# Second MLP layer with its weights stationary, router scores from its column sums, and whole-row gathers for the first two expert blocks

## Chip, cores and metric

One core of a Trainium2 chip runs the kernel. The metric is the device time of one execution in microseconds; times given are medians of several executions, and the profile is of one execution.

## What is computed

Three layers on 1792 tokens of 768 values, in float32. The kernel works with fp32r: a number is split into a high and a low part, and a product is made of three matmuls (high x high, high x low, low x high).

```python
scores = scale * np.matmul(q, k.transpose(0, 1, 3, 2)) - np.log(S)     # 4 x 12 heads, S 448, d 64
attn_out = np.matmul(1.0 / (1.0 + np.exp(-scores)), v)                 # -> x[1792, 768]
h = x @ w_in                                                           # w_in 768 x 2048
x = (np.maximum(h, 0.0) + alpha * np.minimum(h, 0.0)) @ w_out          # w_out 2048 x 768
logits = x @ w_gate                                                    # 8 experts
expert_idx = np.argmax(logits, axis=1)
gate_w = probs[np.arange(N), expert_idx]                               # softmax of the logits
for e in range(E):
    mask = expert_idx == e
    out[mask] = gate_w[mask, None] * (np.maximum(x[mask] @ w1[e], 0.0) @ w2[e])   # F 1024
```

## The kernel before

The five engines are in-order queues: TensorE (PE), VectorE (DVE), ScalarE (ACT), GpSimd (POOL) and SyncE (SP), which issues most DMAs. The order on each is the order in which the program is written (a manual schedule); no planner changes it.

**MLP.** The tokens are four groups, three of 512 and one of 256. The 2048 hidden values are eight chunks of 256. `mlp1` makes h of one chunk and group in columns (hidden value by partition, token along the row) with the weights stationary; ACT and DVE make the activation and split it into `gh` and `gl`. `mlp2` (L365) multiplies by w_out: for each tile of 128 tokens the activation is the stationary operand and 384 columns of w_out are the moving one, two halves of six matmuls (L377 to L379), and DVE adds the result to `acc[ti]`, 128 tokens by 768 (L384). In the last chunk the finished tile is stored to `x2d` in DRAM (L386). `x2d` keeps a token as four quarters of 192 values and one more for the gate.

**Routing.** It is spread between the MLP's last pieces by hooks, calls that run between matmuls. `logits` (L415) takes two tiles at a time: 12 PE transposes (L422), copies by ACT and DVE (L424, L425), 24 matmuls with the router's weights (L432) and one small sum matmul (L438). `choose` (L451) finds the expert, `gates` (L460) the gate; `ranks` (L469) counts tokens by expert with matmuls. The first 8 tiles (groups 0 and 1, the early tokens) are ranked first, so that block 0, 128 tokens of one expert, can be gathered and computed while the rest is routed; the late tiles follow, and then the remaining blocks. `block0_ids` and `block_ids` make lists of token numbers with matmuls; `quarter_rows` (L548) makes of a list the numbers of the quarter rows, with a DVE op that rounds the list to float16 (L556) and four matmuls (L559).

**Experts.** A block is gathered by four indirect DMAs on POOL (`gather`, L723), one for each quarter, so that a DVE transpose of 32 x 32 pieces (`tx`, L747) turns 128 tokens by 768 into columns; ACT and DVE split them (L749, L750). `gate_of` (L729) copies the gates on POOL. `moe1` and `moe2` are the expert's two layers; block 0's are cut in halves (`moe1_halves`, `moe2_halves`) with routing between them. `block_experts` (L597) finds on POOL which expert each block has; ACT, DVE and SP read that row to decide which weights to load and split (`next_w`, `next_split`). `split_w1` and `split_w2` split block 0's and block 1's weights into high and low parts, ACT the high one, DVE the low one (L669 to L691). The tag `raw` has two SBUF buffers, which hold the transposed copies of `logits` and, later, of `tx`.

The order of the main program around the change (L966 to L1075) is: chunks 0 to 5; then mlp1(6,2), router, mlp2(7,1), choose and gates for tiles 0 to 3, mlp1(6,3), router, mlp2(6,2), choose and gates for tiles 4 to 7, mlp1(7,2) with the ranks in its middle, mlp2(6,3) with block 0's ids and gather, mlp1(7,3), mlp2(7,2), mlp2(7,3), the late router work between the halves of expert 0's first layer, the late ranks, its second layer with `block_ids`, gathers of blocks 1 and 2, `block_experts`, and then blocks 1, 2, 3 and on.

## Time and profile before

| what | value |
|---|---|
| median of 3 executions | 950.84 us (950.5 to 951.27) |
| profiled execution | 950.54 us, span 948.5 us from first to last instruction |
| mean granted clock of PE | 0.991 |
| PE busy | 931.7 us, 98% of the span |
| DVE, ACT, POOL busy | 552.5, 353.0, 159.3 us (58%, 37%, 17%) |

The busy time of an engine is the union of its instructions. Matmuls overlap one another, so the duration of one (340 ns with 384 columns) is longer than the distance to the next. The granted clock is the share of TensorE's full clock. Idle time of an engine matters only where PE waits for it, so PE's waits are the thing to read, with the stretches of lower clock.

### The profile page before, as it was taken

The page shows a single profiled execution, that of the slowest core. Times are in us where ns is not written, and L with a number is a line of the kernel's source. Part 1 is how long each engine was busy: PE and PEld are TensorE (multiplying, and loading weights), DVE is VectorE, ACT ScalarE, POOL GpSimd, SP SyncE. Part 2 cuts the span into 40 slices and gives each one's busy share as a digit, 9 for nine tenths or more (in the row PEclk, how much of TensorE's full clock was granted, in tenths as well). Part 3 has the DMA queues.
Part 4 walks back from the last instruction along what each step waited for, and adds up shares of the span by engine and source line. Part 5 has one row for each costly group of instructions (what it writes and reads, how often), then busy time and mean ns, then how long its engine had stood idle before and what let it go on. Part 6 is the DMA issues. An engine that isn't in the chain of part 4 may idle for free. (4 is left out here: it accounts for less than half of the span.)

```text
span 948.5 us, 14230 instructions
## 1 busy us (share of the span) xinstructions
PE 931.7 (98%) x5437; PEld 767.8 (81%) x5437; DVE 552.5 (58%) x976; ACT 353.0 (37%) x561; POOL 159.3 (17%) x210
## 2 busy tenths in 40 slices
PE   9999999999999999999999999898999999999996
PEld 3333338989999899998998989886889989989986
DVE  3454413467777677786867734686397552327841
ACT  5776762223222222223222232343366512116710
POOL 0000000000000000000000000336547362342651
PEclk9999999999999999999999999898999999999999
DMA  7755500011121112112211041730478411057400
GB/s 237 193 202 167 204 1 1 1 50 50 50 67 50 51 55 59 54 52 54 63 50 50 22 96 35 297 86 22 179 298 312 171 61 40 25 182 284 171 19 30
DMA packets 38593, 97.09 MB, mean 102 GB/s; under 512 B 12761, under 2 KB 20825, under 8 KB 35440
## 3 DMA queue, kind: packets, MB, share of 16 engines
...
q8 instruction: 45, 0.74, 0.3%
q14 instruction: 36, 0.29, 0.1%
...
## 5 line engine op out<-in xcount | busy, mean ns | idle before, releaser
L377 PE MATMUL y<-wo,gh 128*128 128x384 f32 x448 | 152.4, 340 | 0.0
L379 PE MATMUL y<-wo,gl 128*128 128x384 f32 x448 | 151.3, 338 | 0.0
L378 PE MATMUL y<-wo,gh 128*128 128x384 f32 x448 | 151.3, 338 | 0.0
L384 DVE TENSOR_TENSOR acc<-y,acc 128x768 f32<-128x768 f32 x98 | 93.2, 952 | 18.3 <-PE y L379 18.3
L353 ACT ACTIVATE r<-h 128x512 f32<-128x512 f32 (+1 forms) x64 | 34.8, 543 | 167.5 <-PE h L351 164.0
L699 POOL MEMSET xg<- 128x772 f32 x4 | 2.9, 744 | 554.5 <-PE xt L422 554.5
L355 DVE SCALAR_TENSOR_TENSOR t<-r,alpha,t 128x512 f32<-128x512 f32 (+1 forms) x64 | 43.8, 684 | 86.5 <-ACT t L354 86.5
L377 PEld LDWEIGHTS y<-wo,gh 128*128 128x128 f32 x448 | 84.5, 189 | 1.2 <-issue 0.4
L378 PEld LDWEIGHTS y<-wo,gh 128*128 128x128 f32 x448 | 84.6, 189 | 0.8
L379 PEld LDWEIGHTS y<-wo,gl 128*128 128x128 f32 x448 | 84.6, 189 | 0.0
L723 POOL DMA_INDIRECT xg<-x2d,rt_qids x72 | 79.0, 1097 | 23.3 <-issue 20.8
L758 PE MATMUL f<-w_b,bh 128*128 128x512 f32 x192 | 77.2, 402 | 3.7 <-ACT bh L749 3.7
L243 ACT ACTIVATE a<-sc,bias 128x896 f32<-128x896 f32 x72 | 67.5, 1015 | 25.9 <-PE sc L252 25.9
L349 PE MATMUL h<-xa,wi 128*128 128x512 f32 x192 | 75.1, 391 | 0.0
L351 PE MATMUL h<-xa,wi 128*128 128x512 f32 x192 | 74.8, 390 | 0.0
L350 PE MATMUL h<-xa,wi 128*128 128x512 f32 x192 | 74.7, 389 | 0.0
L349 PE MATMUL h<-xb,wi 128*128 128x512 f32 (+1 forms) x192 | 65.1, 339 | 0.0
L350 PE MATMUL h<-xb,wi 128*128 128x512 f32 (+1 forms) x192 | 64.9, 338 | 0.0
L351 PE MATMUL h<-xb,wi 128*128 128x512 f32 (+1 forms) x192 | 64.8, 338 | 0.0
L357 DVE TENSOR_TENSOR gl<-t,gh 128x512 fp32r<-128x512 f32 (+1 forms) x64 | 40.1, 626 | 41.4 <-ACT gh L356 41.4
L826 PE MATMUL f<-w,hh 128*128 128x384 f32 x180 | 61.9, 344 | 0.0
L768 ACT ACTIVATE hr<-f 128x1024 f32<-128x1024 f32 x16 | 16.4, 1027 | 119.2 <-PE f L765 83.4
(256 smaller groups left out, 1854.3 us busy)
## 6 DMA issues: line engine op xcount, KB each, us to landing
...
xg<-x2d,rt_qids POOLq DMA_INDIRECT x72
out_dram<-ye,rt_ids POOLq DMA_INDIRECT x18
```

What stands on the lines that cost most here:

```text
L243: nc.scalar.activation(a, pt[:, :, :S], AF.Sigmoid, bias=bias, scale=scale)
L349: nc.tensor.matmul(pt[:, :n], wh[:, ks], a, start=(k == 0), stop=False)
L350: nc.tensor.matmul(pt[:, :n], wh[:, ks], b, start=False, stop=False)
L351: nc.tensor.matmul(pt[:, :n], wl[:, ks], a, start=False, stop=(k == HP - 1))
L355: nc.vector.scalar_tensor_tensor(tj, rj, alpha_sb[:, f:f + 1], tj, op0=ALU.mult, op1=ALU.add)
L377: nc.tensor.matmul(pt[:, nh, :HN], gh[:, j, ts], wh[:, ns], start=(j == 0), stop=False)
L378: nc.tensor.matmul(pt[:, nh, :HN], gh[:, j, ts], wl[:, ns], start=False, stop=False)
L379: nc.tensor.matmul(pt[:, nh, :HN], gl[:, j, ts], wh[:, ns], start=False, stop=(j == 1))
L384: nc.vector.tensor_tensor(dst, pt[:, :, :HN], dst, ALU.add)
L723: nc.gpsimd.indirect_dma_start(out=ex["xg"][b % 4][:, q, :], out_offset=None, in_=rows, in_offset=bass.IndirectOffsetOnAxis(ap=at, axis=0) ...
L758: nc.tensor.matmul(pt[:, n, :], bh[:, k, :], h[n], start=(k == 0), stop=False)
L826: nc.tensor.matmul(pt[:, n, :HN], a, h[:, ns], start=(k == 0), stop=False)
```

## The change

- `mlp2` holds 128 x 128 slices of w_out stationary and moves the activations of a whole group (512 or 256 tokens). The sums come out in columns: `acc[g]` is [128, 6, n], and DVE adds two of the six column chunks at a time (128 x 1024 for 512 tokens).
- `logits` takes a whole group and multiplies the columns directly: no transposes and no copies ahead, 24 matmuls for four tiles, one small sum matmul.
- The rows of `x2d` must now be made. For the 8 early tiles `rows_out` does it on DVE, by a 32 x 32 transpose of 128 x 768 that writes every sixth word, with four stores of 96 KB. For the 6 late tiles `rows_turned` does it on PE (6 transposes) with two ACT copies and one store. Both use the two `raw` buffers.
- `x2d` is [1792, 768]; the gates have a DRAM tensor of their own, and `gate_of` is an indirect DMA of 128 values in place of four POOL copies. Three setup DMAs go.
- Blocks 0 and 1 are gathered by whole rows, one indirect DMA each, and turned by 6 PE transposes with two ACT and two DVE ops. So block 0 needs no quarter ids. The quarter ids of the other blocks, the gather of block 2, `block_experts`, `second_block` and `third_ids` move behind the third of ten runs of block 0's second-layer generator `s2`.
- The hidden-weight splits, the memsets of `xg` and block 0's w2 splits move some places; w1 has another layout in DRAM, and tiles that reused places of `acc` are pieces of the groups.

```diff
-        acc = cx["acc"]
-        t0, n = groups[g]
+        acc = cx["acc"][g]
+        n = groups[g][1]
         gh, gl = gbuf.pop((c, g))
-        for i in range(n // P):
-            ti = t0 // P + i
-            ts = slice(i * P, (i + 1) * P)
-            pt = psum2(f"y{c}_{ti}")
-            for nh in range(2):
-                ns = slice(nh * HN, (nh + 1) * HN)
+        for i in range(HP // 2):
+            pt = psum2(f"y{c}_{g}_{i}")
+            for z in range(2):
+                ks = slice((2 * i + z) * P, (2 * i + z + 1) * P)
                 for j in range(2):
                     wh, wl = w_need("o", 2 * c + j)
-                    nc.tensor.matmul(pt[:, nh, :HN], gh[:, j, ts], wh[:, ns], start=(j == 0), stop=False)
-                    nc.tensor.matmul(pt[:, nh, :HN], gh[:, j, ts], wl[:, ns], start=False, stop=False)
-                    nc.tensor.matmul(pt[:, nh, :HN], gl[:, j, ts], wh[:, ns], start=False, stop=(j == 1))
-            dst = acc[ti].rearrange("p (a n) -> p a n", a=2)
+                    nc.tensor.matmul(pt[:, z, :n], wh[:, ks], gh[:, j, :n], start=(j == 0), stop=False)
+                    nc.tensor.matmul(pt[:, z, :n], wl[:, ks], gh[:, j, :n], start=False, stop=False)
+                    nc.tensor.matmul(pt[:, z, :n], wh[:, ks], gl[:, j, :n], start=False, stop=(j == 1))
+            dst = acc[:, 2 * i:2 * i + 2, :]
             if c == 0:
-                nc.vector.tensor_copy(dst, pt[:, :, :HN])
+                nc.vector.tensor_copy(dst, pt[:, :, :n])
             else:
-                nc.vector.tensor_tensor(dst, pt[:, :, :HN], dst, ALU.add)
-            if c == NCH - 1:
-                nc.sync.dma_start(out=x2d[ti * P:(ti + 1) * P, :, :DQ], in_=acc[ti].rearrange("p (g c) -> p g c", g=G))
-            w_step(2)
+                nc.vector.tensor_tensor(dst, pt[:, :, :n], dst, ALU.add)
+            w_step(3)
...
+    def rows_out(g, i):
+        src = cx["acc"][g][:, :, i * P:(i + 1) * P].rearrange("p k (t j) -> p t k j", j=Q)
+        rows = main.tile([P, G, DQ], F32, tag="raw", bufs=2, name=f"rows{g}_{i}")
+        nc.vector.transpose(rows.rearrange("p t (i k) -> p t k i", k=HP), src)
+        t0 = groups[g][0] + i * P
+        for t in range(G):
+            dst = x2d[t0 + t * Q:t0 + (t + 1) * Q].rearrange("j (g c) -> g j c", g=G)
+            nc.sync.dma_start(out=dst, in_=rows[:, t, :])
...
+    def rows_turned(g, i):
+        src = cx["acc"][g][:, :, i * P:(i + 1) * P]
+        pt = psum2(f"rows{g}_{i}")
+        for k in range(HP):
+            nc.tensor.transpose(pt[:, k // 4, (k % 4) * P:(k % 4 + 1) * P], src[:, k, :], ident)
+        rows = main.tile([P, DM], F32, tag="raw", bufs=2, name=f"rows{g}_{i}")
+        by_chunk = rows.rearrange("p (r k) -> p k r", k=HP)
+        for z, n in ((0, 4), (1, 2)):
+            nc.scalar.activation(by_chunk[:, 4 * z:4 * z + n, :], pt[:, z, :n * P].rearrange("p (k m) -> p k m", k=n), AF.Copy)
+        t0 = groups[g][0] + i * P
+        nc.sync.dma_start(out=x2d[t0:t0 + P], in_=rows)
...
+    def logits(g):
+        acc, n = cx["acc"][g], groups[g][1] // P
+        pl = psum1(f"lg{g}")
+        for k in range(HP):
+            for q in range(n):
+                nc.tensor.matmul(pl[Q * q:Q * (q + 1), :P], wg[:, k, :], acc[:, k, q * P:(q + 1) * P], start=(k == 0), stop=(k == HP - 1))
...
-        nc.vector.tensor_scalar(rt["qid0"], quarter_rows(pid, 1, "qids0"), quarter, None, op0=ALU.add)
...
+    def quarter_ids():
+        pq, idf = psum2("qids")[:, 0, :G * TMAX], rt["idf"]
+        for q in range(G):
+            nc.tensor.matmul(pq[:, q * TMAX:(q + 1) * TMAX], rt["spread"][:, q, :], rt["idh"], start=True, stop=True)
+        nc.vector.tensor_scalar(idf, pq, 0.0, 16384.0, op0=ALU.is_equal, op1=ALU.mult)
+        nc.vector.scalar_tensor_tensor(rt["qids"].rearrange("p q b -> p (q b)"), pq, quarter, idf, op0=ALU.add, op1=ALU.add)
...
+    def indirect_in(dst, src, at):
+        nc.gpsimd.indirect_dma_start(out=dst, out_offset=None, in_=src, in_offset=at, bounds_check=src.shape[0] - 1, oob_is_err=False)
...
+        if b < 2:
+            indirect_in(ex["xg"][b % 4], x2d[:XA if b == 0 else NT], offs(b))
+            return
...
+        indirect_in(rt["gate"][:, b % 4:b % 4 + 1], gated[:XA if b == 0 else NT], offs(b))
...
+        if b < 2:
+            pt = ps2("x", f"tx{b}")
+            for k in range(HP):
+                nc.tensor.transpose(pt[:, k // 4, (k % 4) * P:(k % 4 + 1) * P], xg.rearrange("p (r k) -> p k r", k=HP)[:, k, :], ident)
+            parts = [(pt[:, z, :n * P].rearrange("p (k m) -> p k m", k=n), slice(4 * z, 4 * z + n)) for z, n in ((0, 4), (1, 2))]
+            for src, d in parts:
+                nc.scalar.activation(bh[:, d, :], src, AF.Copy)
+            for src, d in parts:
+                nc.vector.tensor_tensor(bl[:, d, :], src, bh[:, d, :].bitcast(F32), ALU.subtract)
+            return
...
-        mlp2(c1, 1, at(lambda: run(lg[0], lg[2]), lambda: run(lg[0], lg[2]), lambda: run(lg[2])))
+        mlp2(c1, 1, at(lambda: (run(lg[0]), rows_out(0, 0)), lambda: rows_out(0, 1), lambda: rows_out(0, 2)))
         choose(0, 4)
         gates(0, 4)
-        mlp1(c0, 3)
-        run(lg[4])
-        mlp2(c0, 2, at(lambda: run(lg[4], lg[6]), lambda: run(lg[4], lg[6]), lambda: run(lg[6])))
+        mlp1(c0, 3, at(lambda: rows_out(0, 3)))
+        run(lg[1])
+        mlp2(c0, 2, at(lambda: (run(lg[1]), rows_out(1, 0)), lambda: (rows_out(1, 1), rows_out(1, 2)), lambda: rows_out(1, 3)))
...
+        mlp2(c1, 2, lambda i: split_w1(next(split1)))
+        mlp2(c1, 3, at(lambda: split_w1(next(split1)), lambda: (run(lg[2]), rows_turned(2, 0)),
+                       lambda: (split_w1(next(split1)), rows_turned(2, 1))))
+        moe_tiles_h()
+        split2 = iter(range(K2))
+        s1 = moe1_halves(0)
+        run(lg[2])
+        tx(0)
+        rows_turned(2, 2)
+        run(lg[3])
+        split_w1(next(split1))
+        rows_turned(2, 3)
+        run(s1, s1, lg[3])
+        rows_turned(3, 0)
+        rows_turned(3, 1)
         moe_w2()
         for z in range(1, 4):
             new["xg"](z)
+        for _ in range(3):
+            split_w2(next(split2), 0)
+        run(s1, s1, s1, s1)
...
         gather(1)
-        gate_of(0)
-        gather(2)
         for k in range(K2):
             split_w2(k, 1)
-        block_experts()
-        second_block()
-        third_ids()
-        for _ in range(TXAT):
+        for n in range(TXAT):
             run(s2)
+            if n == 2:
+                quarter_ids()
+                gather(2)
+                block_experts()
+                second_block()
+                third_ids()
```

What moves in the engines' queues, at the three places that the prediction speaks of (names with numbers are buffers):

DVE ahead of the early ranks, from the middle of mlp2(6,2) to the op that makes the one-hot experts `rt_oh`, which the ranks read. Before:

```order
L425 COPY xtr_0_4973<-xt_0_4966 128x256
L425 COPY xtr_1_4983<-xt_1_4976 128x256
L384 TENSOR_TENSOR acc_1270<-y_9_4986,acc_1270 128x768
L439 COPY rt_L<-lb_5000 128x16
L384 TENSOR_TENSOR acc_1271<-y_10_5018,acc_1271 128x768
L439 COPY rt_L<-lb_5032 128x16
L384 TENSOR_TENSOR acc_1272<-y_11_5035,acc_1272 128x768
L454 TENSOR_REDUCE rt_mx<-rt_L 128x4
L455 TENSOR_TENSOR rt_eq<-rt_L,rt_mx 128x32
L456 TENSOR_TENSOR rt_eq<-rt_eq,e_65 128x32
L457 TENSOR_REDUCE rt_ix<-rt_eq 128x4
L458 TENSOR_TENSOR rt_oh<-e_65,rt_ix 128x32
```

With the change:

```order
L439 COPY rt_L<-lb_4686 128x32
L385 STREAM_TRANSPOSE rows_0_4689<-acc_1255 128x4x6x32
L374 TENSOR_TENSOR acc_1256<-y_2_1_4695,acc_1256 128x1024
L385 STREAM_TRANSPOSE rows_1_4709<-acc_1255 128x4x6x32
L385 STREAM_TRANSPOSE rows_2_4715<-acc_1255 128x4x6x32
L374 TENSOR_TENSOR acc_1256<-y_2_2_4721,acc_1256 128x1024
L385 STREAM_TRANSPOSE rows_3_4735<-acc_1255 128x4x6x32
L454 TENSOR_REDUCE rt_mx<-rt_L 128x4
L455 TENSOR_TENSOR rt_eq<-rt_L,rt_mx 128x32
L456 TENSOR_TENSOR rt_eq<-rt_eq,e_66 128x32
L457 TENSOR_REDUCE rt_ix<-rt_eq 128x4
L458 TENSOR_TENSOR rt_oh<-e_66,rt_ix 128x32
```

The copies for the router (L425) are gone, and row transposes stand between the adds, three of them between the first add's copy of the scores and the last add, one behind it, all ahead of choose.

POOL from block 1's gather to the start of `block_experts`. Before:

```order
L723 DMA xg_5451<-x2d,rt_qids 128x193 x4
L729 COPY rt_gate<-xg_5153 32x1 x4
L723 DMA xg_5453<-x2d,rt_qids 128x193 x4
L601 TENSOR_TENSOR rt_bend<-rt_bst,rt_nbf 1x8
L602 TENSOR_TENSOR rt_late<-rt_bst,blk 1x168
```

With the change:

```order
L725 DMA pieces_4845<-x2d,rt_ids 128x768
L725 DMA pieces_5237<-x2d,rt_qids 128x192 x4
L600 TENSOR_TENSOR rt_bend<-rt_bst,rt_nbf 1x8
L601 TENSOR_TENSOR rt_late<-rt_bst,blk 1x168
L602 TENSOR_SCALAR rt_late<-rt_late 1x168
```

Block 1's gather is one DMA (128 x 768), the gate copies are gone from here, and block 2's four quarter gathers still stand ahead of `block_experts`.

DVE after `block_ids`. Before, the quarter ids are made at once:

```order
L556 TENSOR_SCALAR rt_idh<-ids 128x21
L586 TENSOR_SCALAR rt_idf<-qids 128x84
L587 SCALAR_TENSOR_TENSOR rt_qids<-qids,quarter,rt_idf 128x84
L589 TENSOR_SCALAR rt_idf<-ids 128x21
L590 SCALAR_TENSOR_TENSOR rt_ids<-ids,rt_idf 128x21
L691 TENSOR_TENSOR w2l_5445<-raw_e,w2h_5444 128x384
```

With the change, the block's token ids come first (just ahead of this piece), and the quarter ids at its end:

```order
L690 TENSOR_TENSOR pieces_5235<-raw_e,pieces_5235 128x384
L1075 TENSOR_TENSOR hl_5141<-th_1_5340,hh_5139 128x512
L690 TENSOR_TENSOR w_0_5229<-raw_e,w_0_5229 128x384
L690 TENSOR_TENSOR w_1_5230<-raw_e,w_1_5230 128x384
L690 TENSOR_TENSOR w_2_5231<-raw_e,w_2_5231 128x384
L690 TENSOR_TENSOR w_3_5232<-raw_e,w_3_5232 128x384
L690 TENSOR_TENSOR w_4_5233<-raw_e,w_4_5233 128x384
L690 TENSOR_TENSOR w_5_5234<-raw_e,w_5_5234 128x384
L690 TENSOR_TENSOR pieces_4847<-raw_e,pieces_4847 128x384
L690 TENSOR_TENSOR pieces_5235<-raw_e,pieces_5235 128x384
L566 TENSOR_SCALAR rt_idf<-qids 128x84
L567 SCALAR_TENSOR_TENSOR rt_qids<-qids,quarter,rt_idf 128x84
```

The quarter ids, which block 2's gather waits for, moved behind the weight subtractions (L690).

## Rows read from the trace of the kernel before

**Rows 1.** The page, part 1: busy us, share of the span, instructions.

```profile
PE 931.7 (98%) x5437; PEld 767.8 (81%) x5437; DVE 552.5 (58%) x976; ACT 353.0 (37%) x561; POOL 159.3 (17%) x210
```

**Rows 2.** List of waits of PE, 540 to 700 us: total, times, longest.

```profile
PE f L758 <- ACT bh L749: 3.7, 1, 3.7
PE qids L559 <- DVE rt_idh L556: 3.4, 2, 3.1
```

**Rows 3.** Busy time by stretch: length, engines, granted clock (PEclk), DMA share, GB/s.

```profile
600.25:607.15 6.90, 5.84 (x25) 5.84 (x26) 3.10 (x12) 0.00 (x0) 3.50 (x4) 0.51 1.01 425
654.85:661.75 6.90, 5.22 (x12) 4.13 (x13) 3.29 (x3) 1.87 (x3) 5.88 (x10) 0.51 0.08 16
547.69:591.33 43.64, 43.64 (x339) 39.66 (x339) 19.75 (x48) 12.69 (x27) 0.74 (x1) 1.00 0.24 57
591.33:630.37 39.04, 35.40 (x259) 33.12 (x258) 24.70 (x58) 12.97 (x23) 15.06 (x15) 0.91 0.65 233
630.37:645.28 14.91, 14.29 (x106) 11.48 (x107) 13.66 (x44) 9.41 (x21) 2.35 (x3) 1.00 0.03 2
645.28:667.37 22.09, 18.00 (x76) 14.91 (x76) 11.66 (x26) 5.73 (x12) 16.87 (x31) 0.85 0.10 23
```

**Rows 4.** Timeline of PE: start us, duration of one or of a run.

```profile
522.75 0.34 PE L377 MATMUL y<-wo,gh 128*128 128x384 f32 x1
...
531.13 0.40 PE L349 MATMUL h<-xa,wi 128*128 128x512 f32 x1
...
539.31 0.34 PE L377 MATMUL y<-wo,gh 128*128 128x384 f32 x1
...
569.64 0.28 PE L349 MATMUL h<-xb,wi 128*128 128x256 f32 x1
...
573.95 1.47 PE L422 MATMUL xt<-ident,acc 128*128 128x128 f32 x12
...
577.44 0.86 PE L432 MATMUL lg<-xtr,wg 128*32 128x128 f32 x24
578.24 1.53 PE L422 MATMUL xt<-ident,acc 128*128 128x128 f32 x12
579.52 0.42 PE L377 MATMUL y<-wo,gh 128*128 128x384 f32 x1
```

**Rows 5.** Groups, lines and one timeline row of DVE, ACT and SP: count, durations (ns by line).

```profile
L384 DVE TENSOR_TENSOR acc<-y,acc 128x768 f32<-128x768 f32 x98 | 93.2, 952 | 18.3 <-PE y L379 18.3
...
L747 DVE STREAM_TRANSPOSE xt<-xg x17: 1542/1640/1682, 654.1 to 916.5; 128x768 f32<-128x768 f32 x17
...
L355 DVE SCALAR_TENSOR_TENSOR t<-r,alpha,t 128x256 f32<-128x256 f32 x4 | 1.9, 485 | 4.0 <-ACT t L354 4.0
...
588.28 0.18 DVE L454 TENSOR_REDUCE rt_mx<-rt_L 128x4 f32<-128x32 f32 x1
...
589.16 0.19 DVE L458 TENSOR_TENSOR rt_oh<-e,rt_ix 128x32 f16<-128x32 f32 x1
...
L424 ACT ACTIVATE xtr<-xt 128x512 f32<-128x512 f32 x14 | 8.0, 594 | 8.4 <-PE xt L422 8.2
...
L386 SPq DMA_DIRECT2D x2d<-acc x14: 512/513/572, 543.8 to 625.5; - x14
```

**Rows 6.** Timeline from block_ids to block 2: PE, POOL, DVE, PE.

```profile
651.17 1.10 POOL L723 DMA_INDIRECT xg<-x2d,rt_qids  x1 [0.30 <-issue]
...
658.40 0.19 POOL L601 TENSOR_TENSOR rt_bend<-rt_bst,rt_nbf 1x8 f32<-1x8 f32 x1
...
665.67 0.29 POOL L618 TENSOR_SCALAR rt_row<-rt_late 1x21 int32<-1x21 f32 x1
...
654.05 1.54 DVE L747 STREAM_TRANSPOSE xt<-xg 128x768 f32<-128x768 f32 x1 [1.63 <-DMA xg<-x2d,rt_qids]
...
656.53 0.79 PE L758 MATMUL f<-w_b,bh 128*128 128x512 f32 x1 [3.68 <-ACT bh L749]
...
667.37 0.40 PE L758 MATMUL f<-w_b,bh 128*128 128x512 f32 x1
```

More of the change, by code (lines that the diff above doesn't have):

```diff
@@ L62 @@
     DQ = DM // G
-    x2d = dram.tile([NT, G, DQ + 1], F32, name="x2d")
+    x2d = dram.tile([NT, DM], F32, name="x2d")
+    gated = dram.tile([NT, 1], F32, name="gated")
     def ctile(name, shape, dt=F32):
@@ L98, in setup_routing @@
         nc.sync.dma_start(out=wg[:, :, 0:E], in_=w_gate)
-        none = pool.tile([P, NTT], F32, tag="none", bufs=1, name="none")
-        nc.gpsimd.memset(none, 0.0)
         yield
-        for g in range(1, G):
-            nc.sync.dma_start(out=x2d.rearrange("(t p) g c -> p t g c", p=P)[:, :, g, DQ:DQ + 1], in_=none.unsqueeze(2))
-            yield
         for n, (dst, src) in enumerate(todo):
@@ L546, in late_places @@
         rt["s"] += place(so, rt["lo"], NE, n - POOLN) + on_pool
-    def quarter_rows(pid, n, name):
-        if "spread" not in rt:
-            rt["spread"] = main.tile([P, G, P], F16, tag="dm", bufs=1, name="spread")
-            nc.vector.tensor_scalar(rt["spread"].rearrange("p q (g s) -> p q g s", g=G),
-                                    slot.rearrange("p (q s) -> p q s", q=G).unsqueeze(2).to_broadcast([P, G, G, Q]),
-                                    part, None, op0=ALU.is_equal)
-        with nc.allow_low_precision(reason="multiples of 4 up to 7168 are exact in float16"):
-            nc.vector.tensor_scalar(rt["idh"][:, :n], pid, float(G), None, op0=ALU.mult)
-        pq = psum2(name)[:, 0, :G * n]
-        for q in range(G):
-            nc.tensor.matmul(pq[:, q * n:(q + 1) * n], rt["spread"][:, q, :], rt["idh"][:, :n], start=True, stop=True)
-        return pq
     def block0_ids():
@@ L590, in block_ids @@
         nc.vector.scalar_tensor_tensor(rt["ids"], pid, -1.0, idf, op0=ALU.add, op1=ALU.add)
+        with nc.allow_low_precision(reason="multiples of 4 up to 7168 are exact in float16"):
+            nc.vector.tensor_scalar(rt["idh"], pid, float(G), None, op0=ALU.mult)
     def third_ids():
@@ L682, in moe_w2 @@
             else:
-                parts.append(tuple(cx["mp"].tile([P, DM], F32R, tag="acc", bufs=NTT, name=f"w2{x}_{k}") for x in "hl"))
+                parts.append(tuple(piece(k - 5, 2 * (k == 6) + z) for z in range(2)))
         ex["w2"] = parts
@@ L691, in split_w2, with piece @@
         nc.vector.tensor_tensor(l[:, s], src, h[:, s].bitcast(F32), ALU.subtract)
+    big = {}
+    def piece(g, i):
+        if g not in big:
+            n = groups[g][1] // P
+            big[g] = cx["mp"].tile([P, n, DM], F32R if g in (1, 2) else F32, tag=f"acc{g}", bufs=1, name=f"pieces{g}")
+        return big[g][:, i, :]
     def moe_tiles_a():
-        acc_t = lambda n, dt, c=DM: cx["mp"].tile([P, c], dt, tag="acc", bufs=NTT, name=n)
         ex["xg"], ex["bx"], ex["y"] = {}, {}, {}
         def xg(z):
-            ex["xg"][z] = acc_t(f"xg{z}", F32, G * (DQ + 1)).rearrange("p (q c) -> p q c", q=G)
+            ex["xg"][z] = piece(*((0, z) if z < 2 else (3, z - 2)))
             nc.gpsimd.memset(ex["xg"][z], 0.0)
         def bx(z):
-            ex["bx"][z] = [acc_t(f"b{x}{z}", F32R).rearrange("p (k m) -> p k m", k=HP) for x in "hl"]
+            ex["bx"][z] = [piece(1 + z, 2 * z + i).rearrange("p (k m) -> p k m", k=HP) for i in range(2)]
         def y(z):
-            ex["y"][z] = acc_t(f"ye{z}", F32)
+            ex["y"][z] = piece(0, 2 + z)
         ex["new"] = dict(xg=xg, bx=bx, y=y)
@@ L741, in tx @@
     def tx(b):
+        xg = ex["xg"][b % 4]
         bh, bl = ex["bx"][b % 2]
[L744 removed]
+        if b < 2:
[8 more added lines that the diff above has]
+            return
+        if "xt" not in ex:
             ex["xt"] = main.tile([P, HP, P], F32, tag="raw", bufs=2, name="xt")
[L746 to L748 removed]
+        t = ex["xt"]
+        nc.vector.transpose(t.rearrange("p k (q s) -> p k q s", q=G), xg.rearrange("p (q i k) -> p k q i", q=G, k=HP))
         nc.scalar.activation(bh, t, AF.Copy)
@@ L949 @@
         cx["mp"] = ctx.enter_context(tc.tile_pool(name="mlp", bufs=1, side="right", reuse_waits="tile"))
-        cx["acc"] = [cx["mp"].tile([P, DM], F32, tag="acc", bufs=NTT, name=f"acc{t}") for t in range(NTT)]
+        cx["acc"] = [cx["mp"].tile([P, HP, n], F32, tag=f"acc{g}", bufs=1, name=f"acc{g}") for g, (_, n) in enumerate(groups)]
         nc.vector.tensor_scalar(alpha_sb, alpha_sb, -1.0, None, op0=ALU.mult)
@@ L961 @@
         routing_tiles()
-        lg = {a: logits(a) for a in range(0, NTT, 2)}
+        lg = [logits(g) for g in range(4)]
         def at(*acts):
```

85 lines of the change are left out of this document (22 added, 63 removed).

## The prediction

> **What bounds the kernel now.** The page comes first: PE is busy 98% of the span [rows 1], so only PE's own work, its waits and its clock can move the time. PE's list of waits between 540 and 700 us comes next. Two matter: 3.1 us (3.4 in two waits) for the quarter ids of block 0, which VectorE (DVE) has not rounded yet, and 3.7 us for block 1's transposed tokens [rows 2]. I call them A and B. The table by stretch shows what else they cost: right behind each, PE runs 6.9 us at a granted clock of 0.51, the lower of its two levels (1.2 of 2.4 GHz), with 5.84 and 5.22 us of it busy. At full clock that work takes half as long, so A and B cost another 2.9 and 2.6 us [rows 3]. All other work up to block 3 is nearly gapless and is priced by the distance between starts [rows 4], not by the longer duration of one matmul.
>
> **MLP second layer.** From 522.75 us on, three stretches follow one another: 48 matmuls of 384 columns, 36 of 512, and 48 of 384 again; the first two took 8.38 and 8.18 us [rows 4]. The change turns the 48x384 of a 512-token group into 36x512, the very shape of the 8.18 us stretch (the first layer's, with weights stationary), so -0.20 us. For the 256-token group 24x384 (half of 8.38, 4.19) become 36x256; such a run took 4.31 us (569.64 to 573.95), +0.12. Per chunk 3 x -0.20 + 0.12 = -0.48, times 8 = -3.8 us: **-3.5** before chunk 6 group 2, -0.4 in the next stage, nothing after it. The Trainium skill, TensorE: Matmul & The Clock Gate, § Back-to-back issue gap, states N/2.4 + 2.5 ns from start to start for an isolated pair; by it 48x384 (7.80 us) and 36x512 (7.77) cost the same, and the edit would give about 0.5 us in place of 3.8 (an estimate from that page). The rows disagree, with 227 ns for 512 columns and 175 for 384, so I take them. DVE's adds grow from 128x768 (0.95 us [rows 5]) to 128x1024, by size 1.27, but three replace four: nothing, while PE is the longer.
>
> **Early routing** (chunk 6 group 2 to the first ranks matmul, 43.64 us [rows 3]). 48 transposes go: 12 took 1.28 us with the switch of type (578.24 to 579.52), so -5.1. Of four sets of 24 router matmuls (0.80 us each, 577.44 to 578.24) two go, -1.6; two small sum matmuls with their switches -0.4; two groups of the second layer -0.4; and +0.5 for copies that now follow the router matmuls at once: **-7.0**.
>
> **A new wait at the ranks.** Before, the last op of choose that the ranks need began at 589.16 and took 0.2, and the ranks started at 591.33, where two stretches meet: 2.0 us to spare [rows 3, 5]. Now eight row transposes stand on DVE ahead of it. The nearest row is the same opcode on the same size, 128x768, 1.54 to 1.68 us; I take 1.58. It reads with a stride and writes densely, the new one reads densely and writes every sixth word: bounds 1.0 us (the 0.95 us add of that size) and 3.2 (twice the row). From the end of the first column pair of chunk 7 group 1, DVE has 6 adds x 1.2, 8 x 1.58, choose (588.28 to 589.35, 1.1), gates (about the same), choose again (1.1), four ops of the 256-token group (0.49 each at most) and about 0.5 of copies: 25.6 us, and some 1.0 of waits for ScalarE and for stores. PE has two pairs (5.5), 36x256 (4.3), router (0.9), 36x512 (8.2), 18x512 (4.1) and small waits (1.0): 24.0. So PE waits **2.6 us** where it had none. Of the stores: four take 4 x 0.51 us to issue on SP [rows 5], and a quarter gather released DVE 1.8 us after its issue had ended (651.17 + 1.10 to 654.05 [rows 6]), so a buffer is free again some 4.2 us after its transpose. There are two, so a third transpose in quick succession waits about 1 us, which is in the 1.0.
>
> **From the ranks to expert 0's first matmul** (39.04 us [rows 3]). A goes: 3.2 of wait, 0.4 of quarter-id matmuls, 2.9 of half clock, -6.5. Late router work: 36 transposes become 24 of rows and 6 of block 0's tokens, and half the router matmuls go, -1.3. New: 2.6 at the ranks; 3.2 of half clock behind it, if the clock falls as at A, some 2.2 us after PE's last start, and for 6.9 us; 1.1 at chunk 6 group 3, whose third pair wants a PSUM buffer that the late DVE still holds; 1.7 at expert 0, where ScalarE's copies of rows (0.59 for 512 columns [rows 5], two a tile) stand before the one that frees its PSUM, held up by the same two buffers; small waits of before, -0.8. Sum **0.0**.
>
> **To the block ids** (14.91 us [rows 3]). Two row tiles (12 transposes) +1.3, router work and its switches -1.4. choose for the late tiles now stands behind ScalarE's copies of tiles (3,0) and (3,1), three weight copies, and DVE's three subtractions: by the same durations 9.6 us from expert 0's start, and PE is there at 6.8: **wait 2.9**, half clock behind it 3.1, old waits -0.6. Sum **+5.3**.
>
> **Blocks 1 and 2.** Call I the end of the block ids, 645.28, where the last two stretches meet [rows 3]. Block 1 started at 656.53 [rows 6], I + 11.25. Now its single gather goes out before any quarter ids (I + 2), lands near I + 4.7, is turned on PE inside expert 0's second half, and block 1 starts near I + 8.5. **B is gone there**, but the next thing is late. Gather 2 now follows quarter ids that stand behind eight weight subtractions, to I + 6.4. Four issues of 1.35 us each end at I + 11.8, and POOL's block_experts then takes 658.40 to 665.96, 7.6 us: the row of experts is ready at I + 19.4, before at I + 20.7. ScalarE's branch reads it, and block 2 started 1.4 us later (667.37); so now I + 20.8 against I + 22.1. PE ends block 1 at I + 16.7: a **new wait of 4.1 us** before block 2, with 2.5 of half clock inside it. Net -1.3 + 2.5 = **+1.2**. Block 3's weights start from the same row of experts, 1.3 us earlier, so they are in time.
>
> **At nothing:** the gate by an indirect DMA (one POOL issue for four copies, wanted a step later), three setup DMAs fewer, 32 stores on SP for 8 (16 us of issue in 28). If a cover fails, 1 to 2 us.
>
> **Sum:** -3.5 - 7.0 + 0.0 + 5.3 + 1.2 = -4.0. The profiled execution took 950.54 us (span 948.5 and 2.0 around it), 0.30 below the median of 950.84. 950.54 - 4.0 = **946.5**.
>
> **Rivals.**
> - *The new waits are too short for the clock to fall* (chance 0.26). They are 2.6 to 4.1 us, and the falls of before came 2.2 to 2.4 us after PE's last start. Without three half-clock stretches (3.2 + 3.1 + 2.5) the time is 937.7; without the waits at the ranks and choose too, 932.2. For it: a transpose nearer 1.0 us. Against: 3.1 us sufficed at A.
> - *DVE bounds the stage before the ranks: slower* (0.18). Place: the eight row transposes, all in line before choose. Each us more of one is 8 us at the ranks. It decides from 4.0 / 8 = 0.5 us more, 2.1 us a transpose; at 3.2 us the time is 959.5. For it: a write stride of 24 bytes, which no row has. The Trainium skill, SBUF — State Buffer, § Door 1: The DMA port swizzle, says that accesses which cross to a new 16-byte line pay a penalty, which is the rule behind this rival. Against: the reads of the row cross likewise, and it took 1.6 us.
> - *The change gives little back* (0.14): the second layer no faster than before, +3.8, and stores that hold their buffer 0.5 us longer: about 950.8.
> - The forecast as worked out: 0.42.
>
> **Numbers.** A measurement of this kernel tells 0.2%, 1.9 us, from no change. Faster: the forecast and the first rival, 0.67 (0.01 of them spill over); same 0.15; slower 0.18. The range goes down to the middle of the first rival, 935.5, and up past no change into the slower one, 953; some 0.2 lies beyond.
>
> **What would show it.** Starts 0.227 us apart in the second layer and 8.18 us a group; the ranks' first matmul 10.5 us earlier than 591.33; PE waits at the ranks, at the late ranks, and at block 2 on ScalarE, none at quarter ids; a granted clock of 0.5 behind each of the three. The forecast is wrong if a row transpose differs from 1.6 us by over 0.5, if a store holds its buffer over 6 us, or if block 1 waits for its gather.

## The result and the profile after

The changed kernel takes **961.59 us** (median of 4 runs, 959.78 to 962.84) against 950.67 for the kernel before in the same comparison: a ratio of 1.0125, with a 95% interval of 1.0098 to 1.0153. It is slower by 10.9 us where 946.5 was forecast, and lies outside the range. The profiled execution took 962.06 us, its span 960.3.

PE is busy for 929.2 us, 2.5 less than before [rows 1]. So the 11.8 us by which the span grew, and 2.5 more, are time in which PE has no work running. PE's list of waits, kernel after, 540 to 700 us (total, times, longest), answers to [rows 2]:

```profile
PE rank L477 <- DVE rt_oh L458: 14.2, 2, 12.3
PE f L778 <- ACTq L923: 3.2, 1, 3.2
PE lg L432 <- ACT t L345: 3.1, 1, 3.1
```

The waits A and B of before (quarter ids, block 1's tokens) are gone, as forecast. In their place PE waits 12.3 us for choose ahead of the ranks, where 2.6 was forecast. The table by stretch, kernel after (columns as in [rows 3]), has the four stretches of [rows 3] (the border between the last two is here the first matmul of the block ids, at 644.40 in the kernel before), then the one from block 2 to block 3, and last the three stretches of lower clock, each begun in one of the new waits or right behind it:

```profile
547.72:588.01 40.29, 37.21 (x264) 30.70 (x262) 20.90 (x31) 7.21 (x16) 0.74 (x1) 1.00 0.17 38
588.01:637.31 49.30, 35.88 (x286) 31.53 (x285) 31.36 (x69) 16.06 (x29) 11.39 (x11) 0.86 0.60 186
637.31:654.38 17.07, 15.25 (x79) 12.54 (x79) 10.07 (x36) 10.91 (x20) 3.76 (x5) 0.90 0.26 93
654.38:674.86 20.48, 16.83 (x98) 14.04 (x97) 10.79 (x28) 6.54 (x15) 12.06 (x24) 0.99 0.10 25
674.86:696.85 21.99, 20.70 (x100) 17.75 (x101) 5.12 (x6) 6.37 (x8) 10.96 (x11) 0.93 0.53 192
...
592.50:606.30 13.80, 5.75 (x22) 4.59 (x22) 9.13 (x28) 1.83 (x4) 0.00 (x0) 0.51 0.31 89
...
647.10:650.90 3.80, 3.80 (x15) 3.15 (x13) 3.35 (x16) 1.09 (x3) 1.42 (x2) 0.55 0.12 5
...
674.50:677.60 3.10, 2.74 (x7) 2.16 (x8) 0.00 (x0) 1.03 (x1) 2.31 (x3) 0.50 0.35 127
```

The stretch from the ranks to expert 0's first matmul grew from 39.04 to 49.30 us: 10.3 us, of a loss of 11.8 in all. What makes DVE late there is told by line 385, the row transposes (durations as min/median/max):

```profile
L385 DVE STREAM_TRANSPOSE rows<-acc x8: 1537/1576/1643, 561.8 to 598.0; 128x768 f32<-128x768 f32 x8
its engine sat idle before it (us, times) until:
  DMA x2d<-rows: 8.5, 4
  issue: 5.8, 1
```

A transpose took 1.58 us, exactly the value taken. But DVE stood still for 14.3 us ahead of five of the eight. DVE's timeline shows where, in three rows behind that of the first transpose (the other two that waited, at 589.66 and 598.03, did so for 1.55 us each):

```profile
561.80 1.62 DVE L385 STREAM_TRANSPOSE rows<-acc 128x768 f32<-128x768 f32 x1
...
570.31 1.54 DVE L385 STREAM_TRANSPOSE rows<-acc 128x768 f32<-128x768 f32 x1 [2.71 <-DMA x2d<-rows]
...
585.42 1.64 DVE L385 STREAM_TRANSPOSE rows<-acc 128x768 f32<-128x768 f32 x1 [5.82 <-issue]
...
593.89 1.54 DVE L385 STREAM_TRANSPOSE rows<-acc 128x768 f32<-128x768 f32 x1 [2.69 <-DMA x2d<-rows]
```

A transpose writes into one of two buffers, and waits until the stores of the tile before the last have landed. So the stores come next. The DMA view from 574 to 590 us (each figure is one of 40 slices of 0.4 us: DMA share in tenths, then GB/s), and SP's timeline:

```profile
DMA  2222244323556125901103213212222222223222
GB/s 92 96 92 92 94 94 94 93 92 84 17 21 43 4 14 0 27 0 2 2 0 10 15 10 10 23 23 79 83 94 92 92 92 94 94 92 113 94 92 92
```

```profile
563.44 10.66 SPq L389 DMA_DIRECT2D x2d<-rows  x12
574.21 0.45 SPq L467 DMA_DIRECT2D gated<-rt_sm  x1
576.67 25.15 SPq L389 DMA_DIRECT2D x2d<-rows  x20
```

Two things are to be seen. The stores run at 92 to 96 GB/s with a quarter of the DMA engines busy, so the 384 KB of a tile (four stores of 96 KB) need some 4.2 us of transfer alone. And from 578 to 585 us almost nothing moves, although stores are queued: a hole that begins 3.8 us behind the issue of the gates at 574.21, the 128 x 4 single floats that now go into `gated`. For comparison, the stores of the kernel before, one per tile, in its DMA view from 543 to 552 us (slices of 0.225 us):

```profile
DMA  0100000007999999999999899999998799999989
GB/s 0 36 0 0 0 0 0 0 0 242 324 297 321 341 318 307 266 208 259 188 178 137 188 215 198 198 225 198 164 130 143 208 253 191 181 147 154 164 201 160
```

The last thing that differs from the forecast is the second layer. Here are starts of its runs, and of the first layer's between them, on PE's timeline, kernel after, chunk 5 (y is the second layer, h the first):

```profile
406.12 0.40 PE L367 MATMUL y<-gh,wo 128*128 128x512 f32 x1
...
414.52 0.29 PE L340 MATMUL h<-xb,wi 128*128 128x256 f32 x1
...
427.25 0.39 PE L340 MATMUL h<-xa,wi 128*128 128x512 f32 x1
...
435.43 0.28 PE L367 MATMUL y<-gh,wo 128*128 128x256 f32 x1
...
439.63 0.39 PE L340 MATMUL h<-xa,wi 128*128 128x512 f32 x1
```

The first layer's 36x512 takes 8.18 us (427.25 to 435.43), the second layer's 8.40 (406.12 to 414.52), and its 36x256 takes 4.20. Nothing is gained against the 8.38 and 4.19 of before [rows 4].

### The profile page after: what moved, and what is told of

Read it like the earlier page. It is cut to its first block, busy times and chain, and to the rows that moved or that the text cites. A ratio compares the mean times of both kernels' runs of the same rounds, so it can differ in the third digit from the quotient of the medians.

```text
span 960.3 us, 13674 instructions
## 1 busy us (share of the span) xinstructions
PE 929.2 (97%) x5199; PEld 723.5 (75%) x5199; DVE 556.8 (58%) x946; ACT 352.4 (37%) x558; POOL 147.5 (15%) x152
## 4 chain that ended last, share of the span: by engine, by line
PE 61%; issue 20%; POOL 8%; DMA 5%; DVE 2%; ACT 1%; SPq 0%; POOLq 0%; DVEq 0%; ACTq 0%
PE h L340 8%; PE h L341 8%; PE h L342 8%; PE y L367 8%; PE y L369 8%; PE y L368 8%; POOL pieces L725 7%; PE av L257 6%; PE sc L243 6%; DMA pieces<-x2d,rt_qids 3%; DMA x2d<-rows 2%; PE av L263 1%; PE sc_r L252 1%; DVE rows L385 1%; ACT rows L400 1%
## 5 line engine op out<-in xcount | busy, mean ns | idle before, releaser
L367 PE MATMUL y<-gh,wo 128*128 128x512 f32 (+1 forms) x384 | 141.3, 368 | 0.8 <-DVE rt_row L1023 0.8
L369 PE MATMUL y<-gl,wo 128*128 128x512 f32 (+1 forms) x384 | 140.5, 366 | 0.0
L368 PE MATMUL y<-gh,wo 128*128 128x512 f32 (+1 forms) x384 | 140.5, 366 | 0.0
L374 DVE TENSOR_TENSOR acc<-y,acc 128x1024 f32<-128x1024 f32 (+1 forms) x84 | 90.7, 1086 | 13.4 <-PE y L369 12.8
L706 POOL MEMSET pieces<- 128x768 f32 x4 | 2.9, 739 | 585.4 <-DVE rows L385 574.5
L367 PEld LDWEIGHTS y<-gh,wo 128*128 128x128 f32 x384 | 72.1, 188 | 14.3 <-DVE acc L374 1.1
L369 PEld LDWEIGHTS y<-gl,wo 128*128 128x128 f32 x384 | 72.0, 188 | 13.2
L368 PEld LDWEIGHTS y<-gh,wo 128*128 128x128 f32 x384 | 72.1, 188 | 12.9
L778 PE MATMUL f<-w_b,pieces 128*128 128x512 f32 x192 | 77.0, 401 | 3.6 <-ACTq L923 3.2
L725 POOL DMA_INDIRECT pieces<-x2d,rt_qids x68 | 73.1, 1075 | 24.7 <-issue 20.4
L340 PE MATMUL h<-xb,wi 128*128 128x512 f32 (+1 forms) x192 | 65.8, 343 | 0.0
L342 PE MATMUL h<-xb,wi 128*128 128x512 f32 (+1 forms) x192 | 65.6, 341 | 0.0
L341 PE MATMUL h<-xb,wi 128*128 128x512 f32 (+1 forms) x192 | 65.5, 341 | 0.0
L849 PE MATMUL f<-w,hl 128*128 128x384 f32 x180 | 60.7, 337 | 0.1
```

The lines of the kernel that those rows point to most:

```text
L340: nc.tensor.matmul(pt[:, :n], wh[:, ks], a, start=(k == 0), stop=False)
L341: nc.tensor.matmul(pt[:, :n], wh[:, ks], b, start=False, stop=False)
L342: nc.tensor.matmul(pt[:, :n], wl[:, ks], a, start=False, stop=(k == HP - 1))
L367: nc.tensor.matmul(pt[:, z, :n], wh[:, ks], gh[:, j, :n], start=(j == 0), stop=False)
L368: nc.tensor.matmul(pt[:, z, :n], wl[:, ks], gh[:, j, :n], start=False, stop=False)
L369: nc.tensor.matmul(pt[:, z, :n], wh[:, ks], gl[:, j, :n], start=False, stop=(j == 1))
```

## The experiments

Two theories of the loss: **S**, the stores of a row tile are slow, as the outermost dimension of their destination is 4 (it is walked as 4 x 32 x 192 values); and **G**, the gates, written as single floats among the row stores, stop them. They don't exclude one another; the question is how much each is worth. For the second layer, what costs 0.22 us a group is asked apart: the order of its operands, their values, or their place. Each kernel was compared with the kernel before on the same chip; where a median is given, the ratio to it has its 95% interval.

### e1_stores: the same rows in stores over 32 partitions

```diff
-        for t in range(G):
-            dst = x2d[t0 + t * Q:t0 + (t + 1) * Q].rearrange("j (g c) -> g j c", g=G)
-            nc.sync.dma_start(out=dst, in_=rows[:, t, :])
+        for g4 in range(G):
+            dst = x2d[t0:t0 + P].rearrange("(t j) (g c) -> g j t c", t=G, g=G)[g4]
+            nc.sync.dma_start(out=dst, in_=rows[g4 * Q:(g4 + 1) * Q])
```

> The four stores of a row tile take a quarter of the partitions each (32 partitions outermost) instead of a quarter of the tokens (4 pieces outermost); bytes, runs of 768 B and their number stay. Theory S (the stores are slow because each moves at 93 GB/s with a DMA share of 0.27, some 4 of 16 engines): the stores move at over 200 GB/s, VectorE's waits for row buffers before its transposes fall from 14.3 us to under 4 in sum, PE's wait at the ranks from 12.3 to 3 to 6, the time to 951 to 955. Theory G (the 4-byte gate writes stall the DMAs for 6 us around 580 us): the 5.8 us wait of the fifth transpose stays, PE waits 6 us or more at the ranks, the time is about 956. Theory V (VectorE has too much to do): nothing changes, 961 to 962.

Median 948.7 us, ratio 0.9992 (0.9977 to 1.0007): with this edit alone, and four stores of 96 KB as before it, the kernel takes the time of the kernel before. Not all of that is the stores' doing. Of the 15.3 us between the profiles of after and e1, 11.3 lie ahead of block 2 (its start moves from 674.86 to 663.59); 3.4 lie between block 2 and block 3, which the edit doesn't touch (see What stays open). The DMA view of 560 to 575 us (slices of 0.375 us), e1 and then the kernel after:

```profile
DMA  0000000000588886007888830488887600600046
GB/s 0 0 0 0 0 0 0 0 0 0 123 195 191 213 199 129 0 0 166 197 195 215 193 84 0 96 189 195 217 195 156 8 0 0 22 0 0 0 115 131
```

```profile
DMA  0000000000001222222222222222222222222222
GB/s 0 0 0 0 0 0 0 0 0 0 0 0 25 51 90 84 55 78 94 66 82 90 82 68 94 92 90 96 90 92 96 90 92 96 90 92 94 92 92 92
```

A tile's stores now run at some 200 GB/s and are done after six slices, with pauses between tiles, where those of after never pause. The waits of e1, in the same view as above:

```profile
PE rank L477 <- DVE rt_oh L458: 7.7, 2, 5.8
...
PE lg L432 <- ACT t L345: 0.3, 1, 0.3
```

The longest wait at the ranks fell from 12.3 to 5.8 us, and the 3.1 us at the router matmuls went with it. S is shown. The rest, 5.8 us against the forecast 2.6, is what G is about: in e1 two transposes still waited 5.0 us for stores. The Trainium skill, DMA: Bandwidth & Descriptors, § Why a DMA increments its semaphore by 16 and not by 1, says that a DMA is spread over the largest number of engines, up to 16, that divides the slowest dimension longer than one on both of its sides: four for `[4][32][192]` from 128 partitions. The traces agree: a DMA share of 0.27 (590 to 598 us of after) at outermost 4, and 0.8 in the fullest slices of e1's view at 32.

### e5_gates_late: the gates in one DMA after the late choose

```diff
-        nc.sync.dma_start(out=gated.rearrange("(t p) c -> p t c", p=P)[:, a:b], in_=sm[:, a:b].unsqueeze(2))
+        if b == NTT:
+            nc.sync.dma_start(out=gated.rearrange("(t p) c -> p t c", p=P), in_=sm.unsqueeze(2))
...
-                gate_of(0)
...
+        gate_of(0)
```

> The gates of all 14 tiles go to DRAM in one DMA after the late choose, and block 0's gate is gathered behind block 1's gather; the slow stores stay. Theory G (the two early 4-byte gate DMAs, issued among the row stores, stop the DMA traffic for some 6 us each): the hole of 576 to 585 us goes, VectorE's wait of 5.8 us before its fifth transpose falls to under 2, PE's wait at the ranks from 12.3 to 7 to 9 us, and block 0's first weights move at once; the time is about 957. [...]

Median 957.84 us, ratio 1.0096 (1.0073 to 1.0119). The DMA view of 574 to 590 us, to be held against that of after:

```profile
DMA  2222222222222242222222222232222222222222
GB/s 92 92 92 92 94 92 94 92 92 92 92 96 93 77 116 56 84 92 92 94 94 92 94 90 92 86 97 92 94 92 92 92 88 92 92 94 94 90 94 94
```

The hole is gone, and the stores stay slow. PE's wait at the ranks:

```profile
PE rank L478 <- DVE rt_oh L458: 8.2, 2, 6.3
PE tx L758 <- issue: 3.4, 1, 3.4
```

So G is shown as well, at 6.0 us of the 12.3. But the median is only 3.8 us lower. In the profile (960.96 us, the longest of four executions) the gain is gone by the start of block 1: from the first matmul of the block ids to there PE takes 15.57 us for 8.59 in after. It has a new wait of 3.4 us at block 1's tokens, behind whose gather `gate_of(0)` now stands, one of 2.1 on ScalarE, and a granted clock of 0.50 for what it does between them. What it is about the gates that stops the stores is not shown: e2 and e3, which were to write them at a pitch of 3076 bytes in place of 4, gave no time.

### e6_stores_gates: both edits

> The late gates and the stores over 32 partitions each. If G holds beside S, PE's wait at the ranks falls from e1_stores' 5.8 us to the 2 to 3 us of the forecast, the traffic runs without holes, and the time is 2 to 4 us under e1_stores' 948.7: 945 to 947. If G is nothing by itself, it equals e1_stores.

```profile
PE rank L478 <- DVE rt_oh L458: 3.6, 2, 1.8
PE tx L758 <- ACT pieces L855: 3.0, 1, 3.0
```

Median 948.12 us, ratio 0.999 (0.9975 to 1.0005). The wait at the ranks is 1.8 us, under the 2.6 forecast, and transposes wait 0.8 us for stores in all. Yet the time is e1's. By the profiles, e6 is 4.5 us ahead of e1 at the block ids (638.04 for 642.54) and 3.7 at block 2 (659.86 for 663.59), and loses 4.4 from there to block 3 (23.04 us for 18.62), in the stretch that is left open below. The wait of 3.0 us ahead of block 1 stands where e1 waits 2.0. There PE wants a PSUM buffer from line 855, ScalarE's product with the gate, and ScalarE waits for the gate (its timeline, e6):

```profile
647.32 0.58 ACT L855 ACTIVATE pieces<-e,rt_gate 128x384 f32<-128x384 f32 x1 [5.41 <-DMA rt_gate<-gated,rt_id]
```

With S and G mended the change is no measurable gain, where the forecast's sum had -4.0.

### e4_order and e7_x_moving, e11_x_values: why the second layer is not faster

e4 gives the second layer the first layer's order of operands, wh·gh, wh·gl, wl·gh:

```diff
-                    nc.tensor.matmul(pt[:, z, :n], wl[:, ks], gh[:, j, :n], start=False, stop=False)
-                    nc.tensor.matmul(pt[:, z, :n], wh[:, ks], gl[:, j, :n], start=False, stop=(j == 1))
+                    nc.tensor.matmul(pt[:, z, :n], wh[:, ks], gl[:, j, :n], start=False, stop=False)
+                    nc.tensor.matmul(pt[:, z, :n], wl[:, ks], gh[:, j, :n], start=False, stop=(j == 1))
```

> In the second layer the three matmuls of a product stand in the first layer's order: high x high, high x low, low x high with the same stationary slice in the first two. Theory O (the order is what makes 36 matmuls of 512 columns take 8.40 us there and 8.18 in the first layer): 8.18 us per 512-token group and 4.31 per 256-token group, chunk 6 group 2 starts 3.5 us earlier, the time falls by 3 to 4 us to about 958. Rival (it is the operands' place or the short accumulation of six): 8.40 and 4.20 stay, and the time stays at 961.6.

The runs stay 8.40 and 4.20 us long, so the order is not it. (The median, 957.5 us, ratio 1.0091 with 1.0062 to 1.0121, is 4 us below after's all the same: see the end of this section.)

e7 moves slices of x in place of gh and gl in chunks 0 to 5, so that the second layer there multiplies other numbers; the layer's real product and the routing are not computed:

```diff
+        if c < NCH - 2:
+            x, o = (xa, groups[g][0]) if groups[g][0] < XA else (xb, groups[g][0] - XA)
+            gh, gl = x[:, 0, 0:2, o:o + n], x[:, 1, 0:2, o:o + n]
```

> In chunks 0 to 5 the second layer moves slices of the first layer's input x in place of the activations (so what it computes is not the layer's result, and the routing that follows is another); the weights, shapes, PSUM places and counts are the same. Theory M (what is moved, its place or its values, sets the 233 ns between starts): with x it is the first layer's 227 ns, 8.18 us per group of 512 and 4.31 per group of 256. Rival W (the stationary slices, or the accumulation of only six): 8.40 and 4.20 stay.

```profile
402.60 0.39 PE L370 MATMUL y<-xa,wo 128*128 128x512 f32 x1
...
410.76 0.28 PE L340 MATMUL h<-xb,wi 128*128 128x256 f32 x1
415.07 0.40 PE L370 MATMUL y<-xb,wo 128*128 128x512 f32 x1
...
423.26 0.39 PE L340 MATMUL h<-xa,wi 128*128 128x512 f32 x1
...
431.42 0.28 PE L370 MATMUL y<-xb,wo 128*128 128x256 f32 x1
435.74 0.40 PE L340 MATMUL h<-xa,wi 128*128 128x512 f32 x1
```

The same weights with x moving: 8.16 and 8.19 us, and 4.32 for 256 columns, the figures of the forecast. (Its whole time, 980.61 us, says nothing: another routing.) That leaves the values of x, or the place that they lie in. e11 fills the tiles gh and gl with the values of x in the same chunks, and leaves out the same:

```diff
-            nc.scalar.activation(hj, tj, AF.Copy)
-            nc.vector.tensor_tensor(gl[:, j, :n], tj, hj.bitcast(F32), ALU.subtract)
+            if c < NCH - 2:
+                nc.scalar.activation(hj, x[:, 0, j, o:o + n].bitcast(F32), AF.Copy)
+                nc.vector.tensor_copy(gl[:, j, :n], x[:, 1, j, o:o + n].bitcast(F32))
+            else:
+                nc.scalar.activation(hj, tj, AF.Copy)
+                nc.vector.tensor_tensor(gl[:, j, :n], tj, hj.bitcast(F32), ALU.subtract)
```

> As the changed kernel, but in chunks 0 to 5 the activations' tiles are filled with the first layer's input (its high and low parts) in place of the activations, so the result and the routing are others; place, shape, order and weights of the second layer stay. With e7_x_moving, where the same values were moved from their own place at 8.16 us per group of 512 columns: theory Values: 8.16 to 8.19 us and 4.31 for 256 columns again. Theory Place (where the activations lie in SBUF, or that engines write nearby): 8.40 and 4.20 as in the changed kernel.

Back at 8.40 us (406.97 to 415.37 on PE's timeline). So it is not the values. That leaves the place in SBUF of the operand that moves, or that engines write there while PE works.

### e8, e9, e10: what PE waits for behind the ranks

Three steps on top of e6. e8 puts the quarter ids, block 2's gather and `block_experts` ahead of the eight weight subtractions:

```diff
+        run(s2)
+        quarter_ids()
+        gather(2)
+        block_experts()
...
-        for n in range(TXAT):
+        second_block()
+        third_ids()
+        for n in range(TXAT - 1):
```

> As e6_stores_gates, and the quarter ids, block 2's gather and block_experts go ahead of block 1's eight weight splits, one run of the second layer's generator after block 1's gather. Forecast's theory of the wait before block 2 (block_experts on POOL is late because gather 2 waits for quarter ids behind the splits): PE's wait on ScalarE there (1.7 to 3.6 us so far) goes or falls under 0.5, block 2 starts 2 to 3 us earlier against block 1, and the time falls 2 to 4 us under e6. Rival (block 3's weights or the clock behind the wait at block 1 take it back): block 3 starts no earlier, the time is that of e6.

Median 948.05 us, ratio 0.9991 (0.9977 to 1.0005): nothing gained. PE's waits of its profile are now 1.7 us for the row of experts, 1.5 for block 1's tokens and, behind block 2's start, 2.9 for its hidden layer from ScalarE. e9 also moves the gather of block 0's gate ahead of block 1's gather:

```diff
+        gate_of(0)
...
-        gate_of(0)
```

> As e8_early_ids, with block 0's gate gathered after the late places and ahead of block 1's gather, where POOL was idle (in e6 and e8 it stood behind block 1's gather, held POOL until 647.4 us and ScalarE's output of block 0 until 648.9). Theory (the gate's place cost the 3 us that e6 lost in front of block 1): PE's waits in front of block 1 fall under 1.5 us in sum, block_experts ends 4 us earlier, block 2 follows block 1 without a wait over 0.5 us; the time is 944 to 946. Rival (block 3's weights or ScalarE's branches take it back): 948.

Median 947.51 us, ratio 0.9978 (0.9966 to 0.9989), where 944 to 946 was expected: PE now waits 3.6 us for block 1's gather. e10 also moves two row transposes and block 0's gather behind the third pair of chunk 6 group 3, so that choose comes first:

```diff
-        mlp2(c0, 2, at(lambda: (run(lg[1]), rows_out(1, 0)), lambda: (rows_out(1, 1), rows_out(1, 2)), lambda: rows_out(1, 3)))
+        mlp2(c0, 2, at(lambda: (run(lg[1]), rows_out(1, 0)), lambda: rows_out(1, 1)))
...
-                gather(0)
...
+            if i == 2:
+                rows_out(1, 2)
+                rows_out(1, 3)
+                gather(0)
```

> As e9_gate_place, with the last two row transposes of the early tiles and block 0's gather behind mlp2(6,3), so that six of eight stand ahead of the early choose. Theory (VectorE's queue ahead of choose is what is left of the ranks' wait, 2.0 us in e6 and e8): that wait goes (3.2 us of transposes less), no half clock behind it, and the time is 2 to 4 us under e9. Rival (VectorE's work only moves: PE waits at block 0's ids or for a PSUM buffer in mlp2(6,3) instead, or block 0's gather is late): the time of e9.

Median 946.82 us, ratio 0.9965 (0.9951 to 0.9978): 0.7 us under e9, where 2 to 4 were expected. Its waits:

```profile
PE tx L758 <- DMA pieces<-x2d,rt_ids: 5.5, 1, 5.5
PE rank L478 <- DVE rt_oh L458: 1.6, 1, 1.6
PE tx L758 <- DMA pieces<-x2d,rt_id: 1.5, 1, 1.5
```

The wait at the first ranks is gone (588.01 to 600.55 in after, 585.89 to 585.93 here), and the one wait of 1.6 us is at the late ones. Block 1's own gather is now the late one, 5.5 us. Block 2 starts at 659.86 us in e6, and at 660.98, 661.53 and 662.41 in e8, e9 and e10: no step brought it forward, as each wait taken away uncovers the next.

### e12_shift96: the halves 96 bytes on

e10, with gh and gl 96 bytes behind a multiple of 128, as the slices of x lie:

```diff
-        gh = mp.tile([P, 2, 512], F32R, tag="gh", bufs=2, name=f"gh{c}_{g}")
-        gl = mp.tile([P, 2, 512], F32R, tag="gl", bufs=2, name=f"gl{c}_{g}")
+        gh = mp.tile([P, 1056], F32R, tag="gh", bufs=2, name=f"gh{c}_{g}")[:, 24:1048].rearrange("p (a n) -> p a n", a=2)
+        gl = mp.tile([P, 1056], F32R, tag="gl", bufs=2, name=f"gl{c}_{g}")[:, 24:1048].rearrange("p (a n) -> p a n", a=2)
...
```

> e10_rows_later with the halves gh and gl of the first layer's product in tiles 128 bytes longer per partition, of which bytes 96 to 4191 are used, so that each half begins 96 bytes behind a multiple of 128, as the slices of x that the first layer moves do, and stays in the same region of SBUF. Theory, the start within 128 bytes decides: a second-layer stretch of 36 matmuls over 512 columns takes 8.16 to 8.18 us instead of 8.40 (and one of 256 columns 4.31 instead of 4.20, as with the slices of x), so that the stretch from the first second-layer group of chunk 0 to the early routing shortens by some 20 x 0.22 - 8 x 0.1 = 3.6 us: median 943.2 us against 946.8. Rival, the region of SBUF decides: the stretches stay at 8.40 and 4.20 and the median at 946.8 within 0.5.

```profile
504.41 0.40 PE L367 MATMUL y<-gh,wo 128*128 128x512 f32 x1
...
512.80 0.39 PE L340 MATMUL h<-xa,wi 128*128 128x512 f32 x1
...
520.97 0.39 PE L367 MATMUL y<-gh,wo 128*128 128x512 f32 x1
...
529.13 0.39 PE L340 MATMUL h<-xa,wi 128*128 128x512 f32 x1
```

Neither theory: of the two buffers that groups take in turn, one became fast (8.16 us, 520.97 to 529.13) and one did not (8.39, 504.41 to 512.80). Engines write both alike, so the place decides. Both begin 96 bytes behind a multiple of 128, so it is not that remainder alone. The remainder by 256 does fit: a tile of 4224 bytes is 16.5 times 256, so of two in a row only one can lie as x does. As placed, the fast buffer and x begin 96 bytes behind a multiple of 256, the slow buffer 224, and both buffers of after, which are slow, 128. No run varied that alone, so a rule stays open. Median 945.48 us, ratio 0.9956 (0.9942 to 0.9971): the lowest time here, 5.0 us under the kernel before in its own comparison. Against e10 it is 1.3 us less, and the two intervals overlap.

### What stays open

From block 2 to block 3 the kernel before, e1 and e4 took 18.6 us, e9, e10 and e12 19.9 to 20.6, and after, e5, e6 and e8 22.0 to 23.3. Part of it can be read in after: 1.5 us are lower clock (3.01 us of work at 0.50 from block 2's start on, behind its wait of 3.2), and 1.2 are two waits of 0.7 and 0.5. e1 and e4 waited 1.7 and 1.8 us at block 2, and the clock did not fall. e5, e6 and e8 have a wait of 2.1 to 2.9 us on ScalarE inside the stretch, and 3.4 us of lower clock behind it. What makes these waits isn't known. SP issues block 3's weights in longer steps in after; one row of its queue each, after and then before:

```profile
675.91 15.79 SPq L647 DMA_DIRECT2D raw_e<-in_w_dram  x9
```

```profile
667.92 11.31 SPq L648 DMA_DIRECT2D raw_e<-in_w_dram  x10
```

Nothing in the edits accounts for which kernels show it: e4 differs from after in the order of two lines, far ahead. Each of these figures is of one execution, and executions of one kernel lie up to 5.3 us apart (946.48 to 951.76 us for the kernel before, in e1's comparison), so the stretch may differ by execution and not by kernel. It is worth some 3.4 us of after's 11.8, and no run tests it.

## Why the prediction was wrong

Step by step (us against before; stretches of the profiled spans, the border between the last two put at the first matmul of the block ids, 644.40 in before and 654.38 in after):

| step | forecast | measured | what differed |
|---|---|---|---|
| up to chunk 6 group 2 | -3.5 | 0.0 | second layer 8.40 and 4.20 a group, not 8.18 and 4.31; chunk 0 began 0.6 earlier (139.86 for 140.41) |
| early routing | -7.0 | -3.4 | the removed work went, 3.1 of new wait at the router matmuls |
| ranks to expert 0 | 0.0 | +10.3 | wait 12.3, not 2.6; lower clock behind it 2.9, not 3.2; 0.2 at expert 0, not 1.7 |
| expert 0 to the block ids | +5.3 | +3.0 | wait 2.0, not 2.9; half clock behind it costs 1.9, not 3.1 |
| block ids to block 2 | +1.2 | -2.5 | wait 3.2, not 4.1; its half clock falls behind block 2 |
| block 2 to the end | 0 | +4.4 | 3.4 of it from block 2 to block 3 (1.5 lower clock, 1.2 two waits, their cause and the rest open), 1.0 spread |

- **The step that failed is the price of the stores.** The prediction put a buffer free "some 4.2 us after its transpose", from four issues of 0.51 us and the 1.8 us after which a quarter gather released DVE. The issues were right (0.52 us, the median). The transfer was not priced: the new destination has 4 as its outermost dimension, and a tile's stores need 4.2 us on a quarter of the engines. A buffer was held for 6.9 us (the first transpose ended at 563.42, and the third, into the same buffer, began at 570.31), and DVE waited 8.5 us on stores. Its own test, "if a store holds its buffer over 6 us", is met.
- **The writes of the gates had no term.** "At nothing" counts the gather of a gate, as a DMA that is wanted a step later; what the writes into `gated` do to the DMAs queued behind them was not asked. One transpose stood 5.8 us in the hole. Stores and gates together make 10.5 of the 12.3 us at the ranks; e6, with neither, has 1.8.
- **The second layer.** The change has "the very shape of the 8.18 us stretch", but not the place of its moving operand: nothing was gained where 3.8 was forecast. The rival "The change gives little back" had that in its condition. The Trainium skill, TensorE: Matmul & The Clock Gate, § Back-to-back issue gap, has a formula for an isolated pair by which both shapes cost the same (7.80 and 7.77 us, the prediction's estimate from it). That they do is what was measured, 8.38 and 8.40 us, though both are higher.
- **Right:** a DVE transpose at 1.58 us (the rival of slow transposes had the right place, DVE ahead of choose, and the wrong cause); A and B gone; a wait at the ranks, at the late ranks, at block 2; the clock at its lower level behind all three, a granted 0.51, 0.55 and 0.50; the third pair's wait, 0.8 us for 1.1; and the early work, in which PE was busy for 37.2 us against the 36.6 forecast.
- **Luck:** the price of the lower clock behind the ranks, 2.9 us for 3.2. The clock was taken to fall 2.2 us after PE's last start and to stay low for 6.9. It fell after 4.5 (588.01 to 592.54) and stayed low for 13.7, but PE worked in only 5.75 of them.
- The chances: "gives little back" and the slow transposes together had 0.32. Neither reached 961.6 (950.8 and 959.5): the only late store among them was put at 0.5 us.
